# First output chunk of an expert inside its last products, six banks, column sums on GpSimd, reordered maxima

## The chip, the core and the metric

One of the eight cores of a Trainium2 chip runs the whole program. The metric is the device time of one execution in microseconds (us). Engines are named as the profile names them: PE is TensorE's matmul, PEld its weight load, DVE VectorE, ACT ScalarE, POOL GpSimd, SP SyncE (here it only issues DMAs).

## What is computed

Banded attention over 2 batches, 8 heads, 768 positions and width 64, whose output is read as 1536 tokens of width 512. Then a mixture of 8 experts, in which every token goes through every expert. Its weights P come from eight rounds of row and column scaling. Then a second mixture, in which every token is given to one expert by a greedy matching with 192 places for each expert.

```python
# first mixture (x: 1536 x 512, w1: 8 x 512 x 1024, w2: 8 x 1024 x 512)
P = np.exp(logits)
for _ in range(8):
    P /= P.sum(1, keepdims=True) + 1e-09
    P /= P.sum(0, keepdims=True) + 1e-09
    P *= N / E
for e in range(E):
    h = np.maximum(x @ w1[e], 0.0)
    out += P[:, e:e + 1] * (h @ w2[e])
# second mixture: tokens in the order of their logits, cap = N // E for each expert
for e in range(E):
    out[assigned == e] = np.maximum(x[assigned == e] @ w1[e], 0.0) @ w2[e]
```

## The kernel before

**Precision.** Each factor of a large product is split into a high and a low half of type f16 after it was scaled by a power of two (`split_hi` on ACT, L814; `split_lo` on DVE, L817), and a product is three matmuls (high-high, high-low, low-high). The scale needs the largest magnitude of the matrix: `maxima` (L1142) loads each matrix once more in eight pieces of 128x512 ("looks"), measures them in turn on ACT (L882) and DVE (L1195), and `settle` (L1199) spreads the result over the partitions by a small matmul (L134) into the bank `PGB` and forms the scale. All lists of such jobs go by `jobs` (L1349 to L1368), and `maxima` may run `AHEAD` = 3 jobs ahead of the splits.

**Stages.** Attention, then the hidden layer of expert 0 as 24 groups of 12 matmuls (L1418, `mm3`, L868 to L870; relu on ACT, L861 and L862, low half on DVE, L863). Beside its last groups run the eight rounds of scaling (L908 to L921): eight DVE operations a round, and the column sum as a matmul with ones (L918) into the bank `bc`. `bc` has the pool tag `misc`, which has one buffer, and so has `PGB` (L1412). Then, for experts 1 to 7, the hidden layer by one level of Strassen's scheme in Winograd's form: `hidden` (L1509) runs six `Set`s (two feature parts y, three token blocks tb), each with seven products of 12 matmuls of 256 columns (L1477). A product into a bank must wait until what lies there has been read: product 3 goes to the bank Y, which the DVE step L1540 reads after product 6. Experts 3 and 4 (`HB` and `HB + 1`) run as one list of twelve sets. The weights for it are in `WS`, one buffer: the parts of expert e + 1 (`kind == "fast"`, L1257; sums of blocks on POOL, L1281 to L1300) may be written only when expert e's sets with the same y are done, which the key `("hidden", e, y)` tells. After the hidden layer, `out_step` (L1599) runs the second product of the expert in 12 chunks of 128 tokens (24 matmuls of 512 columns, L1451) and adds each to `acc` by one DVE step (L1458). It needs W2 of the expert (`"plain"`, L1316 to L1343, tile `wslot`, one buffer), which may be written once the last chunk of the expert before is done. Chunks 0 to 10 stand behind the hidden layer, chunk 11 behind the first products of the next (`beside`). Expert 3's hidden values are put away in HBM, and its chunks as well as all 12 of expert 7 are held back.

**Order.** From L1618 on each engine follows the order of the program (`in_order`). Side work (splits, maxima, gate projections) stands in generators, and `pump` (L1397), which is called between the matmuls, lets them go on: each call adds credit for ACT, DVE and POOL (`CYCLE` in the hidden layer, `CHUNK` in the chunks), and a step is put into the program when its cost is covered. `pause(n)` and `ready` wait for a count that each call raises by 3. `have(key)` puts the side work into the program at once, credit or not, until the key is there.

**Tail.** After `late_logits` (L1057: the gate logits of experts 3 and 7 from their hidden values) come seven rounds of matching (L1746), whose latency is filled with the 24 chunks that were held back: `run(n)` puts n steps of three matmuls (L1668) into the program, eight steps a chunk, 24 steps a round. What is left is run at L1873. Then the second mixture.

Of the kernel before, what the change touches and what calls it, by code (L numbers as in the profile page):

```python
# [20 lines left out]
P = 128  # L21
# [21 lines left out]
def tile_sparse_attention_moe_moe(ctx, tc, q, k, v, ng, nl, wg1, w11, w12, wg2, w21, w22, out, taps=None):  # L43
# [864 lines left out]
    for it in range(8):  # L908
# [49 lines left out]
    AHEAD, SLACK, LAG2 = 3, 20, 28  # L958
    PEEKS = {1: 1, 2: 2, 3: 1, 4: 2, 5: 1}
    now = [0]  # L960
    LAG = 22

    def project(items, when=None):
# [42 lines left out]
        for k in range(-1, n + 1):  # L1006
# [3 lines left out]
            yield 1, 0  # L1010
# [8 lines left out]
            if fresh:  # L1019
                while not when(ahead.c):  # L1020
                    yield None
                yield 1, 0
                m = measure(ahead)
# [4 lines left out]
            yield 0, 2 if here else 0.7  # L1028
# [4 lines left out]
            if fresh:  # L1033
                yield 0, 1.2
                rescale(ahead, m, pt)
# [17 lines left out]
    def partial_logits(e):  # L1053
        yield from project([SimpleNamespace(src=acc[:, c, :], s=None, dst=L[:, c, :], plus=L[:, c, :], c=c, fetch=None)
                            for c in range(NC)], lambda c: ("added", e, c) in done)

    def late_logits(e, tb, plus, beside=None):  # L1057

        while e not in VG:
            yield None  # L1060
# [81 lines left out]
    def maxima(jobs):  # L1142

        n = 8 * len(jobs)
# [3 lines left out]
        def look():  # L1148
            while looks and nxt[0] < n:
                g = nxt[0]  # L1150
                w = source(*jobs[g // 8])
# [13 lines left out]
        for k, (kind, e, which) in enumerate(jobs):  # L1165
            if k < nxt[0] // 8 and 8 * k not in held:
                continue
            while k > at[0] + AHEAD:
                yield None
            if kind == "gate":  # L1170
                while jobs.index(("back", e, which)) not in scales:
# [8 lines left out]
                yield from project([SimpleNamespace(g=8 * k + f, s=scales[jobs.index(("back", e, which))], dst=V[:, f, :], plus=None, fetch=fetch)  # L1180
# [9 lines left out]
            settling.append(Stream(settle(k, jobs[k], am)))  # L1190

    def measured(t, am, a):
        yield (0, 1) if a % 2 else (1, 0)
# [5 lines left out]
    def settle(k, job, am, slack=SLACK):  # L1199
# [7 lines left out]
        yield 0, 1.3  # L1207
        scales[k] = rest()

    def weights(jobs):  # L1210
# [30 lines left out]
        if not wide:  # L1241
# [8 lines left out]
            yield from settle(0, jobs[0], am, 12)  # L1250
        for place, k in enumerate(real):
            kind, e, which = jobs[k]
            at[0] = k
            while k not in scales:
                yield None
            s = scales[k]
            if kind == "fast":  # L1257
                for y in range(NY):
                    while e > 1 and ("hidden", e - 1, y) not in done:
# [19 lines left out]
                    yield 1, 2, 4  # L1279
# [3 lines left out]
                    his((2, b22))  # L1283
                    yield from pause(9)
                    yield 1, 1
                    los((2, b22))
                    his((4, b11))
                    yield from pause(3)
                    yield 1, 1, 2
                    los((4, b11))  # L1290
                    nc.gpsimd.tensor_tensor(b11, b22, b11, op=ALU.subtract)  # L1291
                    his((6, b12))
                    yield from pause(8)
                    yield 1, 1
                    los((6, b12))
                    his((5, b11))
                    yield from pause(3)
                    yield 0, 1, 2
# [742 lines left out]
```

## Time and profile before

| | us |
|---|---|
| median of three runs | 1348.01 (1346.95 to 1348.44) |
| the profiled execution, its own time | 1346.19 |
| its span, first to last instruction | 1344.4 |
| PE busy in the span | 1257.6 (94%) |
| DVE busy | 896.9 (67%) |
| ACT busy | 757.5 (56%) |
| POOL busy | 208.6 (16%) |

The rows below come from this one execution. A row of the order of time begins with start and length in us, then engine, line, operation, output and inputs, and in brackets how long the engine had stood idle before it and which instruction ended that. "xN" joins N instructions of one kind. [...]

### The profile page before, as it was taken

Reading aid. Unit: us, or ns where it says so; the run is one execution under the profiler, and the core shown is the slowest. Engines: PE = TensorE matmul, PEld = TensorE weight load, DVE = VectorE, ACT = ScalarE, POOL = GpSimd, SP = SyncE. Lnnn points to the kernel's source line nnn. Section 1 sums busy time; section 2 is a strip of 40 time slices with the busy share of each in tenths; the row PEclk is TensorE's granted clock in tenths of the full one; section 3 lists DMA queues with packets and bytes.
Section 4 is the critical chain, followed back from the end, with each engine's and each line's share of the span. In section 5 each row is a group of like instructions: output and inputs, shape, how many; then the busy total and the mean of one; then the engine's idle time right before and its main releaser. Section 6 shows DMA issues by size and latency. Waiting matters only on the chain.

```text
span 1344.4 us, 24604 instructions
## 1 busy us (share of the span) xinstructions
PE 1257.6 (94%) x9481; PEld 824.8 (61%) x9481; DVE 896.9 (67%) x2038; ACT 757.5 (56%) x1507; POOL 208.6 (16%) x256
## 2 busy tenths in 40 slices
PE   6899789999999999988999999999997999979998
PEld 4666334586478448877458646955794444457665
DVE  7866684777647744667747765676667898835771
ACT  5866342576346525657537654644564686725872
POOL 2643610401101200211200030020000000031000
PEclk9999989999999999989999999999998999989999
DMA  9540004475732573635687666223737125167760
GB/s 233 122 113 8 1 18 139 141 252 165 242 120 62 172 227 113 226 110 172 191 258 246 193 207 225 84 64 126 235 101 245 64 70 206 48 225 260 250 206 24
DMA packets 155509, 207.19 MB, mean 154 GB/s; under 512 B 56448, under 2 KB 89216, under 8 KB 154240
## 3 DMA queue, kind: packets, MB, share of 16 engines
q1 hardware_dynamic: 153040, 193.04, 45.3%
q0 software_dynamic: 1920, 6.29, 1.3%
q10 hardware_dynamic: 432, 6.29, 1.1%
q8 instruction: 74, 1.21, 0.4%
q14 instruction: 43, 0.35, 0.1%
HBM read 174.13 MB, written 31.46 MB: 153 GB/s over the span
## 4 chain that ended last, share of the span: by engine, by line
PE 69%; issue 12%; DVE 10%; ACT 5%; DMA 2%; POOL 2%; POOLq 0%; SPq 0%; ACTq 0%; DVEq 0%
PE pX L1451 22%; PE pY L1477 9%; PE py L1668 8%; PE pX L1477 7%; PE pV L1477 4%; PE pZ L1477 3%; PE pY L1451 2%; PE pZ L1451 2%; PE ph L868 2%; PE ph L870 2%; PE ph L869 1%; DVE hslot L1498 1%; PE pr L1792 1%; DVE xt L1782 1%; DMA raw<-in_moe_w_dram 1%
## 5 line engine op out<-in xcount | busy, mean ns | idle before, releaser
L1477 PEld LDWEIGHTS <-ws 128*128 128x128 f16 x3528 | 346.2, 98 | 64.8 <-issue 20.7
L1451 PE MATMUL pX<-wslot,hslot 128*128 128x512 f16 x1440 | 317.2, 381 | 5.3 <-ACT wslot L814 2.7
L1451 PEld LDWEIGHTS <-hslot 128*128 128x128 f16 x1728 | 168.5, 98 | 203.7 <-issue 9.8
L1668 PE MATMUL py<-wslot,hslot 128*128 128x512 f16 x576 | 135.1, 384 | 0.0
L1477 PE MATMUL pX<-xt,ws 128*128 128x256 f16 x1008 | 126.7, 275 | 2.1 <-ACT pY L1526 2.1
L1477 PE MATMUL pY<-xs,ws 128*128 128x256 f16 x1008 | 125.7, 274 | 2.0 <-DVE pZ L1555 2.0
L1281 POOL TENSOR_TENSOR raw<-raw 128x512 f32<-128x512 f32 x14 | 23.3, 1664 | 583.2 <-DVE ws L817 381.4
L1498 DVE TENSOR_TENSOR hslot<-relu,hslot 128x512 f16<-128x512 f32 x126 | 88.9, 729 | 37.2 <-ACT relu L1491 36.8
L814 ACT ACTIVATE ws<-raw,s 128x512 f16<-128x512 f32 x98 | 68.3, 718 | 49.1 <-POOL raw L1291 14.7
L1668 PEld LDWEIGHTS <-hslot 128*128 128x128 f16 x576 | 53.6, 99 | 64.8 <-issue 9.4
L817 DVE SCALAR_TENSOR_TENSOR ws<-raw,s,ws 128x512 f16<-128x512 f32 x98 | 84.7, 886 | 10.3 <-ACT ws L814 10.3
L1458 DVE SCALAR_TENSOR_TENSOR acc<-pX,pf,acc 128x512 f32<-128x512 f32 x50 | 37.4, 749 | 71.7 <-PE pX L1451 71.7
L882 ACT ACTIVATE wide<-raw 128x512 bf16<-128x512 f32 x83 | 52.1, 627 | 50.5 <-DMA raw<-in_moe_w_dram 50.0
L1477 PE MATMUL pY<-xt,ws 128*128 128x256 f16 x504 | 63.3, 276 | 12.3 <-DVE s L1540 12.3
L817 DVE SCALAR_TENSOR_TENSOR w2slot<-raw,S,w2slot 128x512 f16<-128x512 f32 x72 | 51.6, 748 | 28.1 <-ACT w2slot L814 27.5
L868 PE MATMUL ph<-xt,w2slot 128*128 128x192 f16 x256 | 62.8, 248 | 6.3 <-ACT relu L862 5.0
L1488 ACT ACTIVATE hslot<-s 128x512 f16<-128x512 f32 x42 | 26.5, 630 | 68.3 <-DVE s L1540 68.2
L1195 DVE TENSOR_REDUCE wam<-raw 128x1 f32<-128x512 f32 x85 | 57.6, 677 | 10.3 <-DMA raw<-in_moe_w_dram 10.1
L814 ACT ACTIVATE w2slot<-raw,S 128x512 f16<-128x512 f32 x72 | 49.2, 722 | 25.1 <-DMA raw<-in_moe_w_dram 20.2
L870 PE MATMUL ph<-xt,w2slot 128*128 128x192 f16 x256 | 62.7, 246 | 0.0
L869 PE MATMUL ph<-xt,w2slot 128*128 128x192 f16 x256 | 62.7, 246 | 0.0
L1477 PE MATMUL pV<-xs,ws 128*128 128x256 f16 x504 | 62.3, 274 | 0.0
(337 smaller groups left out, 2342.5 us busy)
## 6 DMA issues: line engine op xcount, KB each, us to landing
raw<-in_moe_w_dram SPq DMA_DIRECT2D x299, 256.0 KB, 3.4
raw<-in_moe_w_dram SPq DMA_DIRECT2D x60, 512.0 KB, 5.1
relu<-in_moe_w_dram SPq DMA_DIRECT2D x85, 256.0 KB, 2.9
pre<-spill SPq DMA_DIRECT2D x56, 256.0 KB, 4.2
w2slot<-pre SPq DMA_DIRECT2D x4, 2048.0 KB, 8.6
hd<-hslot SPq DMA_DIRECT2D x12, 512.0 KB, 5.2
hslot<-hd SPq DMA_DIRECT2D x12, 512.0 KB, 5.6
w2slot<-pre ACTq DMA_DIRECT2D x3, 2048.0 KB, 15.3
```

What stands on the lines that cost most here:

```text
L814: nc.scalar.activation(hi, raw, AF.Copy, scale=s[:, 0:1])
L817: nc.vector.scalar_tensor_tensor(lo, raw, s[:, 0:1], hi, op0=ALU.mult, op1=ALU.subtract)
L868: nc.tensor.matmul(out_, lhs(0, a), rhs(0, a), start=a == 0, stop=False)
L869: nc.tensor.matmul(out_, lhs(0, a), rhs(1, a), start=False, stop=False)
L870: nc.tensor.matmul(out_, lhs(1, a), rhs(0, a), start=False, stop=a == n - 1)
L882: return nc.scalar.activation(t, src, AF.Abs, accum_out=dst)
L1195: nc.vector.tensor_reduce(am[:, a:a + 1], t, axis=AX.X, op=ALU.max, apply_absolute_value=True)
L1451: nc.tensor.matmul(flat(ps), h[:, y1, f, t * P:t * P + P], w[:, y2, f, :], start=f == 0 and n == 0, stop=f == FC - 1 and n == 2, skip_grou ...
L1458: nc.vector.scalar_tensor_tensor(acc[:, c, :], flat(ps), pf[:, c:c + 1], acc[:, c, :], op0=ALU.mult, op1=ALU.add)
L1477: nc.tensor.matmul(bank[:, u, :], self.w[:, z1, m, c, u * P:u * P + P], x[:, z2, c], start=first and u == 0 and c == 0 and n == 0, stop=c ...
L1498: nc.vector.tensor_sub(lo, r, hi)
L1668: pin(nc.tensor.matmul(ps, h[:, y1, f, t * P:t * P + P], w[:, y2, f, :], start=f == 0 and n == 0, stop=f == FC - 1 and n == 2))
```

## The change

- **Column sums.** L918 on PE becomes one `partition_all_reduce` on POOL, from SBUF to SBUF; the step after it reads SBUF in place of the bank.
- **Chunk 0.** `hidden` gets a call `between`, which runs chunk 0 of the same expert in the last turn of the loop, ahead of the last product 3. For expert 7 two chunks (0 and 1) are now done at this place and behind it; ten are held back.
- **Banks.** The chunks take turns over six banks (X and Y of both parities, V, Z).
- **Weights.** Parts 0, 1, 4 and 5 of the next expert wait for a new key `("early", e, y)`, set after product 5 of the last token block; only parts 2, 6 and 3 wait for `("hidden", e, y)`.
- **Maxima.** The scale of expert 4's first weights is measured ahead of three other jobs (`order`) and may run 6 ahead (`FAR`).
- **Credits.** Costs of small steps go from about 1 to 0.6, and from about 2 to 1.1 or less; `CHUNK` from (0.85, 0.75) to (0.6, 0.5), `CYCLE` from (0.33, 0.38) to (0.28, 0.32); expert 7 no longer has rates of its own.
- **Tail.** All late logits of expert 7 go through the side work (`after` is called for the last two sets too), W2 of expert 7 is loaded beside its first products, and the two calls of `late_logits` behind the loop are gone. Chunk 0 of expert 7 waits until the projection of expert 6 is in the program.

```diff
-        pt = misc([P, E], name="bc")
-        nc.tensor.matmul(pt, ones, pc, start=True, stop=True)
-        nc.vector.tensor_scalar(cs, pt, 1e-9, float(E) / NT, op0=ALU.add, op1=ALU.mult)
+        nc.gpsimd.partition_all_reduce(cs, pc, P, bass_isa.ReduceOp.add)
+        nc.vector.tensor_scalar(cs, cs, 1e-9, float(E) / NT, op0=ALU.add, op1=ALU.mult)
...
-            while k > at[0] + AHEAD:
+            while jobs.index(job) > at[0] + (FAR if kind == "fast" else AHEAD):
                 yield None
...
     def measured(t, am, a):
-        yield (0, 1) if a % 2 else (1, 0)
+        yield (0, 0.6) if a % 2 else (0.6, 0)
...
-                    while e > 1 and ("hidden", e - 1, y) not in done:
+                    while e > 1 and ("early", e - 1, y) not in done:
...
+                    while e > 1 and ("hidden", e - 1, y) not in done:
+                        yield None
+                    yield 2, 0
+                    his((2, b22), (6, b12))
+                    yield from pause(3)
+                    yield 0, 2
+                    los((2, b22), (6, b12))
                     after(2 * y)
...
+    order = list(jobs)
+    x = ("fast", HB + 1, 0)
+    order.remove(x)
+    order.insert(order.index(("gate", HB, 1)), x)
...
-    GROUP, CHUNK, CYCLE = (0.5, 0.5, 0.6, 3), (0.85, 0.75, 1.1, 3), (0.33, 0.38, 0.6, 3)
-    LAST, cycle = (0.3, 0.35, 0.6, 3), list(CYCLE)
+    GROUP, CHUNK, CYCLE = (0.5, 0.5, 0.6, 3), (0.6, 0.5, 1.1, 3), (0.28, 0.32, 0.6, 3)
+    cycle = list(CYCLE)
...
                 s.product(5, s.Y)
+                if s.tb == NTB - 1:
+                    done.add(("early", s.e, s.y))
                 nc.vector.scalar_tensor_tensor(ZB, s.s5, 1.0 / HS1, s.Y, op0=ALU.mult, op1=ALU.add)
                 pump(*cycle)
+            else:
+                after(g)
+                between()
             if j:
                 j.product(3, j.Y)
...
         sets[-1].lower(1, 0, R21)
+        after(sets[-1])
...
         if c == 0:
-            have("plain", e)
+            if e == E - 1:
+                while ("logits", e - 1) not in done:
+                    pump(*cycle)
+            else:
+                have("plain", e)
             factors(e)
-        n = count[0] + c
-        expert_out(e, c, ZB if c == NC - 2 else YB[n % 2] if c == NC - 1 else XB[n % 2])
+        n = count[0] % 2
+        new, old = (XB[n], YB[n]), (XB[1 - n], YB[1 - n])
+        expert_out(e, c, (new[0], old[0], VB, new[1], ZB, new[0], old[0], VB, old[1], ZB, old[0], old[1])[c])
...
+    def beside(e):
+        out_step(e)
+        if e == E - 2:
+            t = wslot(1)
+            nc.sync.dma_start(t, spilled["back", E - 1, 1])
+            W[E - 1, 1] = view(t, 1), W[E - 1, 1][1]
...
-            hidden(make(es), lambda: out_step(prev), after)
+            hidden(make(es), lambda: beside(prev), lambda: out_step(es[-1]), after)
...
-            while len(outs_of[prev]) > 1 and prev < E - 1:
+            while len(outs_of[prev]) > (1 if prev < E - 1 else LEFT):
                 out_step(prev)
...
+            if e == E - 1 and c not in outs_of[e]:
+                continue
...
-    for tb in range(1, NTB):
-        finish(late_logits(E - 1, tb, True, run))
```

## Rows read from the trace of the kernel before

**Rows 1.** Page, first part: busy time, share of the span, instructions.

```profile
PE 1257.6 (94%) x9481; PEld 824.8 (61%) x9481; DVE 896.9 (67%) x2038; ACT 757.5 (56%) x1507; POOL 208.6 (16%) x256
```

**Rows 2.** Busy time by stretch: length, engines (instructions), then PEclk, DMA share, GB/s.

```profile
159.50:193.60 34.10, 25.44 (x107) 11.04 (x106) 29.04 (x75) 11.53 (x25) 13.85 (x9) 0.85 0.03 8
193.50:199.40 5.90, 2.15 (x10) 0.79 (x8) 4.49 (x17) 3.68 (x5) 0.00 (x0) 0.76 0.00 0
200.00:255.00 55.00, 55.00 (x250) 24.71 (x249) 31.51 (x42) 20.82 (x39) 13.30 (x8) 0.97 0.43 138
1016.00:1034.00 18.00, 11.77 (x158) 6.62 (x158) 11.42 (x45) 3.96 (x7) 0.50 (x4) 0.81 0.87 273
```

**Rows 3.** Order of time, PE, from the rounds of scaling to expert 0's first chunk.

```profile
165.66 0.59 PE L918 MATMUL bc<-pc,ones 128*128 128x8 f32 x2 [5.88 <-DVE pc L915]
...
195.06 0.22 PE L134 MATMUL pg<-identh,wam 128*128 128x128 bf16 x1 [0.26 <-DVE cs L919]
198.01 0.59 PE L1451 MATMUL pX<-wslot,hslot 128*128 128x512 f16 x1 [2.73 <-ACT wslot L814]
```

**Rows 4.** Order of time, DVE: one round of scaling, then W2 of expert 0.

```profile
188.80 0.17 DVE L919 TENSOR_SCALAR cs<-bc 128x8 f32<-128x8 f32 x1 [0.48 <-PE bc L918]
...
189.12 0.64 DVE L863 TENSOR_TENSOR hslot<-relu,hslot 128x512 f16<-128x512 f32 x1
...
191.82 0.17 DVE L919 TENSOR_SCALAR cs<-bc 128x8 f32<-128x8 f32 x1 [0.48 <-PE bc L918]
...
197.99 4.87 DVE L817 SCALAR_TENSOR_TENSOR wslot<-raw,s,wslot 128x1024 f16<-128x1024 f32 x4 [0.69 <-ACT wslot L814]
```

**Rows 5.** Order of time, POOL: the folds of the tokens, and its smallest operation.

```profile
145.88 4.59 POOL L1104 TENSOR_TENSOR acc<-xt 128x1024 f32<-128x1024 f16 x2 [6.45 <-ACT relu L862]
...
171.21 2.61 POOL L1110 TENSOR_TENSOR ws<-ws 128x512 f32<-128x512 f32 x2
...
1016.24 0.14 POOL L1705 IOTA rnk<- 128x8 f32 x1
```

**Rows 6.** Groups by line, PE, 200 to 1010 us: busy, mean ns, idle before, releaser.

```profile
L1477 PE MATMUL pY<-xt,ws 128*128 128x256 f16 x492 | 61.8, 276 | 10.8 <-DVE s L1540 10.8
```

**Rows 7.** Order of time, POOL and DVE at the end of expert 4's hidden layer.

```profile
633.68 1.71 POOL L1281 TENSOR_TENSOR raw<-raw 128x512 f32<-128x512 f32 x1 [28.27 <-DVE ws L817]
...
634.19 3.42 DVE L1498 TENSOR_TENSOR hslot<-relu,hslot 128x512 f16<-128x512 f32 x2
```

**Rows 8.** Order of time, DVE and PE where expert 4's sets follow expert 3's.

```profile
568.21 0.69 DVE L1195 TENSOR_REDUCE wam<-relu 128x1 f32<-128x512 f32 x1 [5.02 <-DMA relu<-in_moe_w_dram]
...
573.05 2.72 PE L1477 MATMUL pY<-xt,ws 128*128 128x256 f16 x12 [4.44 <-DVE s L1540]
...
587.27 0.22 PE L134 MATMUL pg<-identh,wam 128*128 128x128 bf16 x1 [2.43 <-DVE L L1091]
...
608.84 2.07 PE L1477 MATMUL pX<-xt,ws 128*128 128x256 f16 x12 [2.06 <-ACT pY L1526]
```

**Rows 9.** Order of time, DVE and PE, W2 of expert 5 and its first chunk.

```profile
756.58 1.47 PE L1477 MATMUL pY<-xt,ws 128*128 128x256 f16 x12 [0.69 <-DVE s L1540]
...
760.73 1.46 PE L1451 MATMUL pX<-wslot,hslot 128*128 128x512 f16 x6 [1.17 <-DVE wslot L817]
...
762.98 1.28 DVE L817 SCALAR_TENSOR_TENSOR wslot<-raw,s,wslot 128x1024 f16<-128x1024 f32 x1
```

**Rows 10.** Order of time, PE, from expert 7's last products to the end of the matching.

```profile
1014.60 1.47 PE L1477 MATMUL pY<-xt,ws 128*128 128x256 f16 x12 [1.51 <-DVE s L1540]
1019.64 0.52 PE L1070 MATMUL pg<-vg7hl,hslot 128*128 128x16 f16 x13 [3.57 <-DVE amax L122]
1027.65 0.56 PE L1070 MATMUL pg<-vg7hl,hslot 128*128 128x16 f16 x16 [1.27 <-DVE L L1091]
1033.41 1.52 PE L1753 MATMUL pw<-ident,rw 128*128 128x128 f32 x12 [1.39 <-DVE rw L1735]
...
1182.14 4.04 PE L1668 MATMUL py<-wslot,hslot 128*128 128x512 f16 x18
```

More of the change, by code (lines that the diff above doesn't have):

```diff
@@ L1027, in project @@
                 pt = spread(m[:, 2:3])
-            yield 0, 2 if here else 0.7
+            yield 0, 1.1 if here else 0.4
             if last:
@@ L1055, in partial_logits @@
                             for c in range(NC)], lambda c: ("added", e, c) in done)
+        done.add(("logits", e))
     def late_logits(e, tb, plus, beside=None):
+        yield None
         while e not in VG:
@@ L1140, in ready, with maxima @@
             yield None
-    def maxima(jobs):
-        n = 8 * len(jobs)
+    def maxima(order):
+        n = 8 * len(order)
         held = {}
@@ L1150, in look @@
                 g = nxt[0]
-                w = source(*jobs[g // 8])
+                w = source(*order[g // 8])
                 c, h = divmod(g % 8, w.shape[1] // 512)
@@ L1164, in maxima @@
         look()
-        for k, (kind, e, which) in enumerate(jobs):
+        for k, job in enumerate(order):
+            kind, e, which = job
             if k < nxt[0] // 8 and 8 * k not in held:
                 continue
-            while k > at[0] + AHEAD:
+            while jobs.index(job) > at[0] + (FAR if kind == "fast" else AHEAD):
                 yield None
             if kind == "gate":
-                while jobs.index(("back", e, which)) not in scales:
+                while ("back", e, which) not in scales:
                     yield None
@@ L1178, in fetch @@
                     yield from ready(begun, LAG2)
-                yield from project([SimpleNamespace(g=8 * k + f, s=scales[jobs.index(("back", e, which))], dst=V[:, f, :], plus=None, fetch=fetch)
+                yield from project([SimpleNamespace(g=8 * k + f, s=scales["back", e, which], dst=V[:, f, :], plus=None, fetch=fetch)
                                     for f in range(FC)])
@@ L1197, in measured, with settle @@
             absmax_bound(t, am[:, a:a + 1])
-    def settle(k, job, am, slack=SLACK):
+    def settle(job, am, slack=SLACK):
         kind, e, which = job
@@ L1206, in settle @@
         yield from pause(6)
-        yield 0, 1.3
-        scales[k] = rest()
+        yield 0, 0.6
+        scales[job] = rest()
     def weights(jobs):
@@ L1249, in weights @@
                 yield from measured(t[:, a % 2 * 512:a % 2 * 512 + 512], am, a)
-            yield from settle(0, jobs[0], am, 12)
+            yield from settle(jobs[0], am, 12)
         for place, k in enumerate(real):
@@ L1415, in tile_sparse_attention_moe_moe @@
     late.append(1)
-    ahead.append(Stream(maxima(jobs)))
+    ahead.append(Stream(maxima(order)))
     flow.append(Stream(weights(jobs)))
@@ L1507, in begin, with hidden @@
         nc.scalar.activation(s.s5, VB, AF.Copy, scale=HS1)
-    def hidden(sets, beside, after):
+    def hidden(sets, beside, between, after):
         n = len(sets)
```

39 lines of the change are left out of this document (15 added, 24 removed).

## The prediction

> **What bounds the kernel now.** I read the busy times first: PE works 94% of the span, no other engine above 67% [rows 1]. So only time in which PE stands still, or runs at the low clock, can be won, and the change must be costed gap by gap. The table of stages says where the gaps are not: from 200 to 255 us PE is busy 55.00 of 55.00 us [rows 2], a stretch of output chunks. It also gives the price of a matmul of 512 columns there: 55.00 / 250 = 0.22 us, so a chunk of 24 takes 5.3 us. Next I read PE's order of time for every row that has an idle time in brackets. Five places hold nearly all of them between 159 and 1190 us, and the change touches each.
>
> First, the rounds of scaling. Between 159.5 and 193.6 us PE is busy 25.44 of 34.10 us at a granted clock of 0.85, and in the 5.9 us behind it 2.15 [rows 2]. PE is in order, the column sum L918 stands among the groups of expert 0, and the first waits 5.88 us for DVE [rows 3]. Then the matmul L134, which gives the scale of W2, runs only at 195.06, behind the last reader of the column sums: its bank has the pool tag of theirs. So W2 is split late (DVE from 197.99 [rows 4]) and the first chunk starts at 198.01 after a wait of 2.73 [rows 3]. Second, the ends of the hidden layers: product 3 waits for L1540, 10.8 us in all [rows 6], 4.44 of it inside the list of experts 3 and 4 [rows 8]. Third, that list. Fourth, W2 of expert 5 [rows 9]. Fifth, the start of the matching [rows 10].
>
> **The change part by part.** The sum is made against the profiled execution's own time, 1346.19 us.
>
> *A, column sums.* Removed: 16 records of L918 and the shared bank. In the stretch from 159.5, 107 records less those 16 are 91 products of expert 0 [rows 2]; at 0.22 they take 20.0 us and end at 179.5, three preparing matmuls later 180.2. Against 198.0 that is a gain of at most 17.8 us, if W2 is split by then. Its scale no longer waits for the rounds, and its split costs DVE 4.87 us [rows 4], so this is possible. Added: eight sums on POOL. No row shows an operation of POOL across partitions. The nearest rows bound it at 0.14 us (the small iota) and 2.3 us (half of the pair of folds, 128x1024) [rows 5]. I take 2.0, near the large one, because the value of each partition has to reach all others. A gain below 0.14 is out, as a sum cannot cost less than POOL's smallest operation. A round takes 191.82 - 188.80 = 3.02 us now, 0.48 of it waiting for PE [rows 4]; the rest, 2.54, holds one L863. With 2.0 a round takes 4.5. The first sum is asked for at 165.6 [rows 3], so the eighth is there at 165.6 + 2.0 + 7 x 4.5 = 199.1, and the factors some 2.4 us later (201.5). Chunk 0 needs them only when its bank is used again, by chunk 5, at 180.2 + 5 x 5.3 = 206.7: five chunks cover it now, where two banks covered two. What may spoil it is DVE, which is in order: the step behind each sum waits, and behind it stand L863 of the groups and the low halves of W2, for which PE waits. If DVE's order holds one L863 a round as now [rows 4], the eight groups left take 8 x 4.5 = 36 us and the chunk starts at about 205, 7 us later than now. The order is made by the scheduler and not in the trace. Bounds -17.8 and +7; I take -10, nearer to the gain, because the groups no longer share PE's order with the sums, and so need not go one a round.
>
> *B, chunk 0 inside.* It puts 5.3 us of PE work between product 6 and product 3. DVE is late there by 10.8 - 4.44 = 6.4 us over the lists [rows 6, 8], for instance because two L1498 took 3.42 us beside two block sums of POOL [rows 7]. No single lateness outside the list of twelve comes near 5.3. Bounds -6.4 and 0 (if the chunk's own side work pushes DVE back as much); I take -6. The bank of chunk 0 is that of the other parity, long read, and costs nothing.
>
> *C, early weights and urgent maxima.* At 568 DVE waited 5.02 us for a look that had only just been loaded: the weights of expert 4 were not ready, the side work was put in at once, and its reads followed their loads too closely. This cost PE 4.44, and the rest of that rush 2.43 and 2.06 [rows 8], together 8.9. Four of seven parts can now be written about one set earlier. But the same splits still fall into the same sets on DVE, so I take -5; bounds -8.9 and 0.
>
> *D, W2 of expert 5.* Chunk 0 is now wanted where product 3 would start, at 756.58 - 0.69 = 755.9; it reaches the last quarter of W2 18 x 0.22 = 4.0 us later, at 759.9, and that is there at 762.98 + 1.28 = 764.3 [rows 9]: 4.4 us of waiting against the 1.17 shown and two smaller ones, some 1.8. If the splits come as now, +2.6; if what was saved in C brings them forward, -1.8; if the lower credits put them back by another 4 us, +7. I take +2.
>
> *E, tail.* From 1016 to 1034 PE has one chunk (5.3) and 128 small matmuls (some 3.5) to do in 18.0 us, at a granted clock of 0.81 [rows 2]: about 9 are lost, plus the 1.51 ahead of product 3 [rows 10]. Two chunks move ahead of the matching: chunk 0 covers the 1.51, chunk 1 the wait for the last relu. Of the 16 steps that leave the tail, 8 stood in this stretch and 8 at its end, where 18 matmuls ran 4.04 us behind everything else [rows 10]; the matmul work is the same. The late logits no longer wait for the bank (3.57) nor for each other (1.27). The chain from the last logits to the first transposes (1.39 today [rows 10]) stays and is less covered, and the end of the matching then waits for DVE's index arithmetic. Bounds -11 and -3; I take -7. W2 of expert 7 is loaded from SP's queue behind chunk 11 of expert 6; the looks queued behind it wait for that chunk, and no matmul waits for them. I cost it at nothing; if a split stood behind it, a chunk's 5.3 us.
>
> *F, credits.* Costs and credits fall together in the hidden layer, so the splits keep their pace. In the chunks they slow down, under ten chunks of cover (53 us). Nothing, except under D.
>
> Sum: -10 - 6 - 5 + 2 - 7 = -26, so 1320.2 for such an execution. The median of the runs shown is 1.8 above it (1348.01 against 1346.19): 1322.
>
> **The rivals.** *Slow sums, slower kernel.* The mechanism is that of A: DVE's order holds one L863 a round, and a sum is longer than the rows suggest. The chunk then starts at 168.6 + 8 x (2.54 + T). The other parts give 16, so the point from which the kernel is slower lies at a start of 214, T = 3.1 us. With T = 5 it starts at 229, 31 us late: 1348 - 16 + 31 = 1363. For it: 2.0 is a guess, and one L863 a round is what the row shows. Against it: the rows of POOL's plain work are all below 2.3, and both conditions must hold.
>
> *First sum late.* POOL is in order too, and its folds run until 171.21 + 2.61 = 173.8 [rows 5], 8.2 us behind the request. If they keep their place, the cover of 206.7 - 201.5 = 5 us takes most of it; if the low halves stand behind, all 8 count: 1330. [...]
>
> *W2 becomes the wait.* The lower credits bring W2 late to more than one chunk 0: +7 at expert 5 in place of +2, and some 5 at expert 1, which has the fewest spare sets: 1332. For it: D has no slack today.
>
> *All of it.* A at -17.8, B at -6.4, C at -8.9, D at 0, E at -9: 42 us, 1306.
>
> *It does nothing.* The gaps come back behind the chunks, because DVE, busy 29.04 of 34.10 us in the rounds [rows 2], is what bounds there: 1348.
>
> **How the numbers follow.** Forecast 1322 with its own range of 1312 to 1331: 0.45. First sum late (1330): 0.10. W2 (1332): 0.14. All of it (1306): 0.10. Nothing: 0.07. Slow sums: 0.14. The range goes from 1304 to 1345; it leaves out the slow sums and most of the case of nothing, about 2 in 10. Within 0.2%, 2.7 us, is about what a measurement of this kernel cannot tell from no change. Faster: 0.45 + 0.10 + 0.14 + 0.10 = 0.79; same 0.07; slower 0.14.
>
> **What would show it.** A: the start of the first chunk (L1451 before) near 180 to 190, the time of one sum on POOL, and whether any chunk waits for its bank. B: no idle time ahead of product 3 with L1540 as its releaser. C: no wait above 1 us between the sets of experts 3 and 4. D: the wait for W2 ahead of expert 5's chunk 0. E: the time from expert 7's last product to the first transposes of the matching, and no matmuls of the held chunks behind the inverse. A sum of over 3 us, or a first chunk after 205, would make the prediction wrong.

## The result, and the profile of the changed kernel

| | before | changed |
|---|---|---|
| median, us | 1347.48 (1346.18 to 1348.44) | 1324.14 (1321.99 to 1327.00) |
| ratio, 95% interval | 1 | 0.9829 (0.9808 to 0.9850) |
| profiled execution, own time | 1346.19 | 1324.13 |

Forecast was 1322. The sum is close, but its terms are not: A gave a third of what it was put at, and B and C together more than they were put at. The page's first part stands against [rows 1]:

```profile
PE 1245.2 (94%) x9465; PEld 819.7 (62%) x9465; DVE 889.4 (67%) x2038; ACT 754.1 (57%) x1507; POOL 207.0 (16%) x264
```

The span fell by 22.1 us (1344.4 to 1322.3), and PE's busy time by 12.4 of these (1257.6 to 1245.2); the other 9.7 us are idle time. PE lost the 16 records of the column sums, which by themselves were busy 3.5 us. Some 6.3 us are the clock (an estimate): the two traces show granted clocks of 1.00 and 0.50 alone; at 0.50 PE was busy for 34.4 us before and for 21.9 us in the changed kernel, and matmuls that came 0.43 us apart at 0.50 came 0.215 apart at 1.00 (the first groups behind the scale of W2, below). The rest, some 2.6 us, is not traced.

**Where it went.** I cut both executions at the same steps of the program: the start of expert 1, of the list of experts 3 and 4, of expert 5, of expert 7, and the first measure behind the matching. Busy time by stretch, before (columns: length, then busy time and instructions of PE, PEld, DVE, ACT and POOL, PEclk, which is the granted clock as a share of full speed, DMA share, GB/s):

```profile
261.49:505.85 244.36, 241.07 (x1692) 160.79 (x1691) 158.24 (x285) 130.58 (x252) 25.63 (x17) 1.00 0.56 177
505.85:700.03 194.18, 182.59 (x1498) 134.42 (x1497) 123.06 (x238) 110.12 (x219) 26.08 (x16) 0.97 0.56 179
700.03:952.50 252.47, 247.42 (x1788) 166.29 (x1787) 168.39 (x342) 140.06 (x274) 23.35 (x16) 1.00 0.53 168
952.50:1188.04 235.54, 224.21 (x1790) 131.19 (x1789) 186.96 (x486) 151.02 (x238) 8.68 (x28) 0.99 0.36 129
```

and the same stretches of the changed kernel:

```profile
258.06:501.36 243.30, 240.91 (x1691) 160.81 (x1690) 154.70 (x282) 128.45 (x248) 24.78 (x17) 1.00 0.53 168
501.36:682.70 181.34, 177.86 (x1499) 132.11 (x1498) 127.55 (x242) 109.49 (x222) 23.33 (x16) 1.00 0.61 201
682.70:936.38 253.68, 249.34 (x1801) 167.58 (x1800) 167.98 (x355) 143.69 (x282) 22.90 (x16) 0.99 0.57 178
936.38:1165.96 229.58, 222.62 (x1778) 130.59 (x1776) 183.09 (x473) 147.04 (x229) 8.57 (x28) 0.99 0.33 120
```

Up to expert 1 the gain is 3.4 us, in experts 1 and 2 it is 1.1, in the list of experts 3 and 4 12.8, in experts 5 and 6 a loss of 1.2, in expert 7 and the matching 6.0. What follows is unchanged (156.4 and 156.3). In the list, idle time fell from 11.59 to 3.48 and busy time from 182.59 to 177.86 for the same work. The reason for the second is the clock: in the list PE was busy at 0.50 for 9.2 us before and never in the changed kernel, and half of that is 4.6. In the kernel before, around the wait of 4.44 us that ends at 573 us [rows 8]:

```profile
560.00:568.00 8.00, 8.00 (x125) 7.34 (x123) 3.08 (x8) 4.11 (x9) 0.00 (x0) 1.00 0.78 241
568.00:576.00 8.00, 3.56 (x21) 2.48 (x19) 6.50 (x19) 2.97 (x7) 0.00 (x0) 0.75 0.56 208
576.00:588.00 12.00, 9.57 (x125) 8.10 (x124) 7.29 (x20) 5.87 (x12) 2.92 (x2) 0.88 0.64 221
```

The granted clock was 1.00 ahead of the wait and 0.50 from 572.0 to 578.8 us, that is for the last us of the wait and the 5.8 us of matmuls behind it. The twelve at 573.05 took 2.72 us [rows 8], a product in the changed kernel takes 1.47.

**The start of the chunks.** PE's order of time, against [rows 3]:

```profile
182.05 0.29 PE L134 MATMUL pg<-identh,wam 128*128 128x128 bf16 x1 [14.73 <-DVE wam L1204]
182.13 0.63 PE L868 MATMUL ph<-xt,wslot 128*128 128x512 f16 x1
...
197.65 10.52 PE L1459 MATMUL pX<-wslot,hslot 128*128 128x512 f16 x48
```

The first chunk (L1459 now) starts at 197.65, before at 198.01. The waits of the rounds became one of 14.73 us at L134, the scale of W2, with the groups queued behind it; and the first twelve matmuls behind it came 0.43 us apart, at a granted clock of 0.50, and those from 187.5 on 0.215, at 1.00. POOL's order of time shows the cause, against [rows 5]:

```profile
166.89 5.09 POOL L1105 TENSOR_TENSOR ws<-xt 128x1024 f32<-128x1024 f16 x2
177.76 0.43 POOL L917 PARTITION_ALL_REDUCE cs<-pc  x1 [5.79 <-issue]
```

The first sum was asked for at 166.06 (the end of DVE's L915 below). POOL had folds until 171.98, and then stood 5.79 us with no instruction and nothing that it waited for. A sum itself takes 0.43 us here and mostly 0.40 later. DVE waited with it, against [rows 4]:

```profile
164.56 1.14 DVE L913 TENSOR_TENSOR Pm<-Pm,rs 128x96 f32<-128x96 f32 x1
165.73 0.33 DVE L915 TENSOR_REDUCE pc<-Pm 128x8 f32<-128x96 f32 x1
...
178.22 0.17 DVE L918 TENSOR_SCALAR cs<-cs 128x8 f32<-128x8 f32 x1 [8.22 <-POOL cs L917]
...
181.88 0.11 DVE L1204 TENSOR_REDUCE wam<-wam 128x1 f32<-128x8 f32 x1
```

Between the last two rows stand, among others, four looks (L1197), and L1204 is what L134 waits for.

**The other places.** Product 3 waits no more for the block sum (L1548 now), against [rows 6]:

```profile
L1485 PE MATMUL pY<-xt,ws 128*128 128x256 f16 x504 | 62.8, 273 | 0.0
```

In the list of experts 3 and 4 the wait of 4.44 us is gone; two are left nearly as they were (2.43 and 2.06 before), against [rows 8]:

```profile
564.02 0.22 PE L134 MATMUL pg<-identh,wam 128*128 128x128 bf16 x1 [1.87 <-DVE L L1092]
...
595.98 1.47 PE L1485 MATMUL pX<-xt,ws 128*128 128x256 f16 x12 [1.62 <-ACT pY L1534]
```

Chunk 0 of expert 5 waits for W2, against [rows 9], PE and then DVE:

```profile
743.34 3.39 PE L1459 MATMUL pX<-wslot,hslot 128*128 128x512 f16 x8 [1.98 <-DVE wslot L817]
```

```profile
744.39 1.27 DVE L817 SCALAR_TENSOR_TENSOR wslot<-raw,s,wslot 128x1024 f16<-128x1024 f32 x1
```

And the tail, PE, against [rows 10]: product 3 of expert 7 and the first transposes of the matching have no wait ahead of them, and no held-back chunk stands behind the inverse.

```profile
1005.79 1.47 PE L1485 MATMUL pY<-xt,ws 128*128 128x256 f16 x12
...
1009.95 0.83 PE L1071 MATMUL pg<-vg7hl,hslot 128*128 128x16 f16 x27 [1.13 <-DVE hslot L1506]
1010.64 4.69 PE L1459 MATMUL pX<-wslot,hslot 128*128 128x512 f16 x21
1015.17 1.04 PE L1774 MATMUL pw<-ident,rw 128*128 128x128 f32 x8
```

### The profile page after: what moved, and what is told of

It is laid out like the page before. It is cut to its first block, busy times and chain, and to the rows that moved or that the text cites. A ratio compares the mean times of both kernels' runs of the same rounds, so it can differ in the third digit from the quotient of the medians.

```text
span 1322.3 us, 24576 instructions
## 1 busy us (share of the span) xinstructions
PE 1245.2 (94%) x9465; PEld 819.7 (62%) x9465; DVE 889.4 (67%) x2038; ACT 754.1 (57%) x1507; POOL 207.0 (16%) x264
## 4 chain that ended last, share of the span: by engine, by line
PE 68%; issue 11%; DVE 9%; ACT 6%; POOL 3%; DMA 2%; POOLq 0%; ACTq 0%; DVEq 0%
PE pX L1459 11%; PE pY L1485 10%; PE pX L1485 7%; PE pY L1459 7%; PE py L1691 6%; PE pZ L1459 5%; PE pV L1459 5%; PE pV L1485 4%; PE pZ L1485 3%; PE ph L868 1%; DMA raw<-in_moe_w_dram 1%; PE ph L869 1%; PE ph L870 1%; PE pr L1813 1%; ACT ex L610 1%
## 5 line engine op out<-in xcount | busy, mean ns | idle before, releaser
L1459 PEld LDWEIGHTS <-hslot 128*128 128x128 f16 x1776 | 173.3, 98 | 204.0 <-issue 7.0
L1459 PE MATMUL pX<-wslot,hslot 128*128 128x512 f16 x768 | 175.3, 384 | 2.0 <-DVE wslot L817 2.0
L1691 PE MATMUL py<-wslot,hslot 128*128 128x512 f16 x528 | 121.0, 379 | 0.0
L1283 POOL TENSOR_TENSOR raw<-raw 128x512 f32<-128x512 f32 x14 | 24.9, 1778 | 526.8 <-DVE ws L817 399.9
L1459 PE MATMUL pY<-wslot,hslot 128*128 128x512 f16 x432 | 97.0, 379 | 0.0
L817 DVE SCALAR_TENSOR_TENSOR ws<-raw,s,ws 128x512 f16<-128x512 f32 x98 | 77.7, 824 | 15.4 <-ACT ws L814 15.1
L814 ACT ACTIVATE ws<-raw,s 128x512 f16<-128x512 f32 x98 | 65.6, 716 | 37.6 <-POOL raw L1291 18.7
L1197 DVE TENSOR_REDUCE wam<-raw 128x1 f32<-128x512 f32 x84 | 56.8, 678 | 14.2 <-DMA raw<-in_moe_w_dram 14.2
L1459 PE MATMUL pV<-wslot,hslot 128*128 128x512 f16 x288 | 64.7, 379 | 0.0
L1459 PE MATMUL pZ<-wslot,hslot 128*128 128x512 f16 x288 | 64.4, 379 | 0.0
## 6 DMA issues: line engine op xcount, KB each, us to landing
w2slot<-pre SPq DMA_DIRECT2D x4, 2048.0 KB, 12.2
```

Source lines behind the costliest of these rows:

```text
L814: nc.scalar.activation(hi, raw, AF.Copy, scale=s[:, 0:1])
L817: nc.vector.scalar_tensor_tensor(lo, raw, s[:, 0:1], hi, op0=ALU.mult, op1=ALU.subtract)
L1197: nc.vector.tensor_reduce(am[:, a:a + 1], t, axis=AX.X, op=ALU.max, apply_absolute_value=True)
L1283: nc.gpsimd.tensor_tensor(b11, b12, b11, op=ALU.subtract)
L1459: nc.tensor.matmul(flat(ps), h[:, y1, f, t * P:t * P + P], w[:, y2, f, :], start=f == 0 and n == 0, stop=f == FC - 1 and n == 2, skip_grou ...
L1691: pin(nc.tensor.matmul(ps, h[:, y1, f, t * P:t * P + P], w[:, y2, f, :], start=f == 0 and n == 0, stop=f == FC - 1 and n == 2))
```

## Experiments

All were timed in three rounds beside the kernel before, so kernels are compared by their ratios to it (0.001 is 1.35 us). "First chunk" and "list" are read from the profiled execution, "list" being the time from the start of expert 3 to that of expert 5.

| kernel | median | ratio, interval | first chunk | list |
|---|---|---|---|---|
| before | 1347.48 | 1 | 198.01 | 194.2 |
| changed | 1324.14 | 0.9829 (0.9808 to 0.9850) | 197.65 | 181.3 |
| e1_warm | 1327.46 | 0.9857 (0.9839 to 0.9874) | 198.61 | 181.4 |
| e2_hold_last | 1322.79 | 0.9826 (0.9809 to 0.9843) | 194.63 | 181.6 |
| e3_hold_two | 1312.72 | 0.9757 (0.9739 to 0.9775) | 186.27 | 181.7 |
| e4_sums_alone | 1345.76 | 0.9991 (0.9979 to 1.0003) | 197.80 | 193.8 |
| e5_no_between | 1336.31 | 0.9913 (0.9883 to 0.9943) | 197.76 | 185.7 |
| e6_no_urgent | 1319.05 | 0.9789 (0.9773 to 0.9806) | 196.70 | 179.9 |
| e7_late_key | 1322.45 | 0.9817 (0.9801 to 0.9834) | 197.84 | 180.4 |
| e8_own_bank | 1327.34 | 0.9858 (0.9842 to 0.9875) | 195.44 | 181.5 |
| e9_neither | 1326.17 | 0.9839 (0.9823 to 0.9856) | 197.59 | 181.3 |
| e10_old_credits | 1333.41 | 0.9891 (0.9870 to 0.9912) | 199.40 | 181.1 |
| e11_both | 1309.88 | 0.9723 (0.9706 to 0.9739) | 186.46 | 179.3 |
| e12_none_of_three | 1327.28 | 0.9846 (0.9826 to 0.9866) | 199.12 | 182.9 |

### Part A: why was the first sum late?

**e1_warm**: is the delay paid once in a program, or at each change?

```diff
     nc.vector.memset(ones, 1.0)
+    warm = sml.tile([P, E], F32, name="cs")
+    nc.gpsimd.partition_all_reduce(warm, ones[:, :E], P, bass_isa.ReduceOp.add)
```

> One column sum more, of a constant, as POOL's first work of the program; the rest is the changed kernel. Theory (the delay of 5.79 us ahead of the first sum is paid at each change between POOL's ordinary work and its sums): the copies and folds in between bring the delay back, the first sum of the rounds again begins some 5.8 us behind the last fold (at 177.8 us), the first chunk at 197 to 199, the time within 2 us of the changed kernel, 1322 to 1326. Rival (the delay is paid once in a program): the first sum of the rounds begins right behind the fold at 172.0, the wait of PE falls from 14.7 to some 9 us, and the time to about 1318.

POOL, order of time:

```profile
168.96 5.09 POOL L1107 TENSOR_TENSOR ws<-xt 128x1024 f32<-128x1024 f16 x2
180.00 0.43 POOL L919 PARTITION_ALL_REDUCE cs<-pc  x1 [5.95 <-issue]
```

The delay is there again in full, 5.95 us behind the fold, although a sum had run before: it is paid at the change. The warm sum itself holds up attention (POOL's first scaling step begins at 16.36 in place of 11.02), so all these rows stand 2.1 us later. At the first chunk 0.96 of that is left; what else makes up the 3.3 us by which the median lies above the changed kernel's, and 1.5 above the theory's range, was not followed. The compiled order of POOL in the changed kernel has an instruction without operands ahead of the sums, and one ahead of the next ordinary work.

```
65 L1105 TENSOR_TENSOR ws<-xt 128x1024 x2
66 L917 ISA
67 L917 ISA cs<-pc 128x8 x8
68 L1283 ISA
69 L1283 TENSOR_TENSOR raw<-raw 128x512
```

Neither is in the order of time. Under the line of the sums (L917) the trace has two MODIFY_POOL_CONFIG of 6 ns in POOL's queue, at 171.9 and 172.0, where the delay begins, and under L1283 two of 88 ns at 206.4, behind the last sum. That the delay belongs to them is read from their place alone. The delay was 5.79 us in the changed kernel and 5.95 in e1, and e1 adds that POOL's ordinary work in between brings it back.

**e2_hold_last** and **e3_hold_two**: if the sum's lateness is what PE waits for, it can be taken away. The folds of the last token block (e2: `tb >= 2`) or of the last two (e3: `tb >= 1`) are put behind the sums on POOL, so that the delay begins earlier; in e3 it should fall into time in which POOL is idle.

```diff
-        nc.gpsimd.partition_all_reduce(cs, pc, P, bass_isa.ReduceOp.add)
+        summed = nc.gpsimd.partition_all_reduce(cs, pc, P, bass_isa.ReduceOp.add)
...
+            with tc.issue_after(summed.ins) if tb >= 1 else ExitStack():
-            nc.gpsimd.tensor_tensor(R[g], x[:, 0, KH * g:KH * g + KH], x[:, 1, KH * g:KH * g + KH], op=ALU.add)
+                nc.gpsimd.tensor_tensor(R[g], x[:, 0, KH * g:KH * g + KH], x[:, 1, KH * g:KH * g + KH], op=ALU.add)
```

> The changed kernel with the last token block's pair of folds put behind the eight sums on POOL. Theory (the first sum is late by 5.1 us of folds and 5.8 us of delay behind them, and PE's wait follows it one for one): the folds end at 166.9, the first sum begins at 172.7, PE's wait of 14.7 us falls to about 9.6, the first chunk begins at about 192.5 and the time is about 1319. Rival (DVE's own work, not the sum, sets the chunk): first chunk at 197 to 198, time within 1.5 us of 1324.

> The changed kernel with the folds of the last two token blocks put behind the eight sums. Theory (as before, and the delay runs while POOL is idle): the folds of the first block end at 157, the delay of 5.8 us is over by 163, the first sum begins at 166.1 when it is asked for, PE's wait falls from 14.7 to 3 or 4 us, the first chunk begins at 185 to 188 and the time is 1311 to 1315. Rival (the folds are only moved): some 16 us of folds behind the sums hold back the splits of the folded tokens and with them expert 1, which gives more than half of it back: 1319 or more. Rival (DVE sets the chunk): 1324.

e2, POOL, PE and DVE:

```profile
172.35 0.43 POOL L917 PARTITION_ALL_REDUCE cs<-pc  x1 [5.83 <-issue]
```

```profile
179.14 0.29 PE L134 MATMUL pg<-identh,wam 128*128 128x128 bf16 x1 [12.21 <-DVE wam L1205]
```

```profile
172.81 0.17 DVE L918 TENSOR_SCALAR cs<-cs 128x8 f32<-128x8 f32 x1 [5.75 <-POOL cs L917]
...
176.66 0.17 DVE L918 TENSOR_SCALAR cs<-cs 128x8 f32<-128x8 f32 x1
...
178.93 0.15 DVE L1205 TENSOR_REDUCE wam<-wam 128x1 f32<-128x8 f32 x1
```

The sum came when expected (172.35 against 172.7), but PE's wait fell to 12.2 and not to 9.6. DVE's order is made anew for each kernel, and here a second round stands between the first sum and L1205. So the theory of one for one was too simple: PE waits for the sum and for whatever DVE's order puts between it and the scale. The first chunk starts 3.0 us earlier, but the time is that of the changed kernel within the intervals.

e3, POOL, then PE:

```profile
162.75 0.43 POOL L917 PARTITION_ALL_REDUCE cs<-pc  x1 [5.66 <-issue]
165.85 0.40 POOL L917 PARTITION_ALL_REDUCE cs<-pc  x1 [2.68 <-DVE pc L915]
...
199.94 5.09 POOL L1106 TENSOR_TENSOR acc<-xt 128x1024 f32<-128x1024 f16 x2 [7.39 <-issue]
```

```profile
171.57 0.23 PE L134 MATMUL pg<-identh,wam 128*128 128x128 bf16 x1 [4.08 <-DVE wam L1205]
...
186.27 10.52 PE L1460 MATMUL pX<-wslot,hslot 128*128 128x512 f16 x48
```

The wait is 4.08 us and the chunk starts 11.4 us earlier. The folds run at 200 us, and expert 1 starts at 246.68 against 258.06, also 11.4 earlier, so nothing is given back there. At the end the gain is 9.7 us by the ratios (11.4 by the medians).

Holding the folds back did more than empty POOL's queue. DVE's order of time in e3:

```profile
159.91 0.26 DVE L913 TENSOR_TENSOR Pm<-Pm,rs 128x96 f32<-128x96 f32 x1
160.20 0.32 DVE L915 TENSOR_REDUCE pc<-Pm 128x8 f32<-128x96 f32 x1
```

Without folds beside it L913 takes 0.26 us in place of 1.14, and DVE asks for the first sum at 160.52, 5.5 us earlier than in the changed kernel. The delay is not hidden in full, for the sum begins at 162.75, 2.2 us after that. So the sum is 15.0 us earlier, by 5.5 us of earlier request and 9.5 us of shorter lateness (11.7 to 2.2); how much of the 11.4 each of the two brought is not separated. A's 10 us were there to be had: the folds, which stood in POOL's queue and beside which DVE's steps ran slowly, and the delay took them.

**e4_sums_alone**: the kernel before, and of the change only the column sums (the first hunk of the diff).

> The kernel before with only the column sums moved to GpSimd; nothing else of the change. Theory (the first sum is late, so that the move alone brings little): the first chunk begins at 196 to 200 and the time is 1344 to 1348, at most 3.4 us below the kernel before, which is what the changed kernel had gained when expert 1 began. Rival (the move was worth the 10 us of the prediction, and the other parts gave less than they seem to): about 1337.

PE, order of time:

```profile
185.35 0.29 PE L134 MATMUL pg<-identh,wam 128*128 128x128 bf16 x1 [16.41 <-DVE wam L1201]
...
209.51 2.75 PE L1450 MATMUL pX<-wslot,hslot 128*128 128x512 f16 x12 [1.19 <-DVE acc L1455]
```

Alone, A is worth 1.2 us (between a gain of 2.8 and a loss of 0.4). The third chunk waits 1.19 us for its bank, since two banks cover two chunks and the factors come late; with six banks no chunk of the changed kernel waits.

**e8_own_bank**: could the sums have stayed on PE, in the unused fourth part of the scales' bank?

```diff
-        nc.gpsimd.partition_all_reduce(cs, pc, P, bass_isa.ReduceOp.add)
-        nc.vector.tensor_scalar(cs, cs, 1e-9, float(E) / NT, op0=ALU.add, op1=ALU.mult)
+        pt = PGB[:, 3, :E]
+        nc.tensor.matmul(pt, ones, pc, start=True, stop=True, skip_group_check=True)
+        nc.vector.tensor_scalar(cs, pt, 1e-9, float(E) / NT, op0=ALU.add, op1=ALU.mult)
```

(`PGB` is allocated ahead of the rounds.)

> The changed kernel with the column sums on TensorE again, but into the unused fourth part of the bank of the scales, so that the matmul for the scale of W2 needs no bank that the rounds hold. Theory (in the kernel before the shared bank held up W2, and GpSimd was not needed to free it): the sums cost 0.5 us each, nothing waits for folds or for a delay, the scale of W2 is there at 172 to 182, the first chunk begins at 186 to 191 and the time is 1312 to 1318. Rival (the groups of expert 0 share PE's order with the sums, and lose there what the bank gives): first chunk at 196 to 200, 1322 to 1327.

PE, order of time:

```profile
192.68 0.22 PE L134 MATMUL pg<-identh,wam 128*128 128x128 bf16 x1 [0.26 <-DVE cs L920]
195.44 0.59 PE L1460 MATMUL pX<-wslot,hslot 128*128 128x512 f16 x1 [2.54 <-ACT wslot L814]
```

L134 still ran only behind the last reader of the sums, though its operand was there at 176.7: in the program it stands behind the eighth sum and waits for DVE. Here a part of the bank did not act as a bank of its own, so this run doesn't test the theory; whether sums on PE in a truly separate bank would do as well as e3 stays open.

### Parts B, C and F: what freed the lists?

**e5_no_between**: chunk 0 back behind the hidden layer.

```diff
-            hidden(make(es), lambda: beside(prev), lambda: out_step(es[-1]), after)
+            hidden(make(es), lambda: beside(prev), lambda: None, after)
```

> The changed kernel with chunk 0 of each expert back behind the hidden layer; all else as changed. Theory (the chunk hides the lateness of DVE ahead of the last product 3 of every list, and a wait there costs more than its own length because the clock is low behind it): the waits of product 3 for the block sum come back, 6 us or a little more over the lists, and 1 to 3 us of low clock: 1330 to 1333. Rival (the lower credits and the new order of the weights have made DVE early, so that the place of the chunk no longer matters): 1323 to 1326.

Groups of PE, 200 to 1010 us, and busy time by stretch (columns as above):

```profile
L1485 PE MATMUL pY<-xt,ws 128*128 128x256 f16 x498 | 61.9, 273 | 6.7 <-DVE s L1548 6.7
```

```profile
258.17:504.66 246.49, 242.58 (x1691) 161.22 (x1690) 153.33 (x282) 128.84 (x247) 24.78 (x17) 0.99 0.52 166
504.66:690.34 185.68, 179.71 (x1499) 132.53 (x1498) 130.07 (x244) 109.67 (x222) 23.78 (x16) 0.99 0.60 196
690.34:947.34 257.00, 249.87 (x1800) 167.54 (x1799) 166.50 (x347) 142.11 (x279) 23.78 (x16) 0.99 0.54 170
947.34:1181.39 234.05, 225.03 (x1779) 131.47 (x1777) 185.22 (x479) 148.53 (x233) 8.60 (x28) 0.98 0.35 123
```

6.7 us of waits at product 3 are back, close to the 6.4 that the prediction counted for B. But the profiled execution is 15.3 us longer than that of the changed kernel, 8.9 of idle time and 6.5 of busy time (the four stretches against the same four of the changed kernel); the medians differ by 12.2 and the ratios by 11.3. The busy time is the clock: in these stretches PE is busy at 0.50 for 20.2 us, in the changed kernel for 6.8, and half of the difference, which is what the upper level would save, is 6.7. The theory of a wait and its low clock holds; even its upper end of 9 was too low, in part because the last logits of expert 7 wait 3.24 us in e5 and 1.13 in the changed kernel.

**e6_no_urgent**, **e7_late_key**, **e9_neither** (both edits together): which half of C freed the list of experts 3 and 4?

```diff
-            while jobs.index(job) > at[0] + (FAR if kind == "fast" else AHEAD):
+            while jobs.index(job) > at[0] + AHEAD:
...
-    order.remove(x)
-    order.insert(order.index(("gate", HB, 1)), x)
```

```diff
-                    while e > 1 and ("early", e - 1, y) not in done:
+                    while e > 1 and ("hidden", e - 1, y) not in done:
```

> The changed kernel with the maxima in the order of the kernel before, 3 jobs ahead; the early key stays. Theory (it was the look loaded too late that made the wait of 4.44 us at 573 us in the kernel before, and the low clock behind it): a wait of 3 us or more comes back in the middle of the list of experts 3 and 4, this list takes 5 to 9 us longer and the time is 1329 to 1333. Rival (the early key alone freed that list): 1323 to 1326.

> The changed kernel with parts 0, 1, 4 and 5 of the weights waiting for the old key again, the last product 3 in place of product 5; the maxima stay reordered. Theory (the urgent maxima made the gain in the list of experts 3 and 4; the key moves writes by less than one set): 0 to 2 us slower, 1324 to 1326. Rival (the key matters, since four of seven parts come one set later and the rush ahead of expert 4 is back): a wait of 2 us or more between the sets of experts 3 and 4, 1328 to 1332.

> The changed kernel with both undone: the maxima in the order of before, 3 jobs ahead, and the old key for parts 0, 1, 4 and 5. Theory (either of the two is enough to keep the looks ahead of the splits, which is why undoing one alone cost nothing): the wait of 3 to 5 us for a late look comes back in the list of experts 3 and 4, which takes 5 to 9 us longer than in the changed kernel: 1329 to 1333. Rival (neither did it; the lower costs and rates, or the new order of the parts, freed that list): 1317 to 1324 and no wait above 2 us there.

e6, busy time of experts 1 and 2; then PE in the changed kernel:

```profile
257.10:497.45 240.35, 240.35 (x1692) 160.93 (x1691) 156.68 (x285) 129.70 (x250) 24.34 (x17) 1.00 0.54 174
```

```profile
443.50 0.17 PE L992 MATMUL pg<-wg2hl,xp 128*128 128x16 f16 x1 [1.44 <-DVE V L1003]
```

My theory fell twice. Without the reordered maxima the list is no longer but shorter (179.9 against 181.3), and the time falls by 5.4 us (0.9789 against 0.9829, where the intervals just don't overlap). The larger part of it lies ahead of the list: experts 1 and 2 take 240.35 us, in which PE is never idle, against 243.30 in the changed kernel, where PE waits for the gate projection (L992). That projection, for expert 3, is the first of four jobs that the change moved the looks at expert 4's weights ahead of; the same 240.35 come back in e11. Without the key, 180.4 and no difference that can be told. Without both, 181.3 and 1326.17, 1.3 us by the ratios, inside the intervals, and a time between the two ranges on record. The key is of use only where the maxima keep their old order (0.9789 against 0.9839, 6.7 us). DVE does wait for a late look in e6, 3.72 and 4.17 us, but PE loses 0.49 us behind the first and nothing behind the second: in this order little that PE needs stands close behind the look. In e7 and e9 no such wait is above 1.8 us.

**e10_old_credits** and **e12_none_of_three** (e9 and e10 together): was it the credits, which I had costed at nothing?

```diff
-    GROUP, CHUNK, CYCLE = (0.5, 0.5, 0.6, 3), (0.6, 0.5, 1.1, 3), (0.28, 0.32, 0.6, 3)
+    GROUP, CHUNK, CYCLE = (0.5, 0.5, 0.6, 3), (0.85, 0.75, 1.1, 3), (0.33, 0.38, 0.6, 3)
...
-        yield (0, 0.6) if a % 2 else (0.6, 0)
+        yield (0, 1) if a % 2 else (1, 0)
```

(and the other small costs of `project` and `settle` as before)

> The changed kernel with the costs and rates of the credits as before: 1 and 1.3 in place of 0.6 for a look and a scale, the rates of chunks and cycles back. Theory (costs that fell more than the rates let the looks run ahead, which the prediction costed at nothing): the list of experts 3 and 4 takes 4 us or more longer than the 181.3 us of the changed kernel, and the time is 1328 to 1334. Rival (credits change nothing on the path, as the prediction had it): 1321 to 1326.

> The changed kernel with three things undone together: the order of the maxima, the old key, and the costs and rates of the credits. Left of the change are the column sums, chunk 0 inside, the six banks, the tail and the new order of the parts of the weights. Theory (the reordered maxima and the cheaper credits each keep the look of expert 4's weights ahead, so that undoing one of them alone leaves the list of experts 3 and 4 as short as it is): DVE waits again 3 us or more for a look in that list, the list takes 187 to 192 us in place of 181.3, and the time is 1338 to 1344. Rival (none of the three matters there; the new order of the parts, with fewer and shorter pauses, frees it): the list takes 180 to 183 us, no wait for a look above 1.5 us moves PE, and the time is 1331 to 1336.

e10, busy time of experts 1 and 2; then PE:

```profile
259.81:507.71 247.90, 243.50 (x1692) 161.61 (x1691) 157.60 (x285) 130.85 (x253) 23.60 (x16) 0.99 0.53 170
```

```profile
749.99 0.29 PE L134 MATMUL pg<-identh,wam 128*128 128x128 bf16 x1 [4.58 <-DVE wam L1204]
```

e10 is slower by 8.4 us, within my range, but not where I said: the list takes 181.1. In the profiled executions experts 1 and 2 lose 4.6 us (247.90 against 243.30), experts 5 and 6 2.3, the part up to expert 1 and that of expert 7 1.7 each. The longest wait, 4.58 us, stands inside chunk 0 of expert 5, at the matmul for the scale of expert 6's first weights, whose looks came late. e12 has the list at 182.9 and takes 1327.28, less than either theory gave; no look in the list makes DVE wait 0.6 us.

So the old credits cost 8.4 us beside the reordered maxima and 0.9 (not measurable) without them and the key. Undone together, these edits of C and F cost 2.3 us, inside the intervals. The list stays short without them. Of its 12.8 us, chunk 0 inside accounts for 4.3 (e5), and the sums alone leave it at 193.8 (e4). The remaining 8.5 us fall, by elimination only, to what e12 also keeps: the new order of the weights' parts, with shorter pauses, which I think likeliest, the six banks and the edits of the tail. No kernel had one of these alone, and it stays open.

**e11_both**: e3 and e6 together.

> The folds of the last two token blocks behind the sums, and the maxima in the order of the kernel before with 3 jobs ahead; all else as changed. Theory (the two gains lie in different stretches, 150 to 260 us and 375 to 680 us, and add up): 1312.7 - 5.1 = 1307.6, between 1306 and 1310, the first chunk at 186. Rival (an earlier start of expert 1 takes the room that the looks had): 1311 to 1315.

1309.88, 1.1% below the changed kernel and 2.8% below the one before: the fastest version of all. The gains add up in the main (between e3 and e11 4.6 us by the ratios and 2.8 by the medians, against 5.4 for e6), and of the list's 179.31 us PE is busy for 177.58:

```profile
487.21:666.52 179.31, 177.58 (x1497) 132.01 (x1496) 128.12 (x237) 108.68 (x218) 24.07 (x16) 1.00 0.60 198
```

## Why the prediction was right, and where it was wrong

The time (1322 against 1324.14) and the sign were right, with errors that cancelled. Step by step, from the profiled executions:

- **A** failed: -10 was put down, the first chunk came 0.4 us earlier, expert 1 started 3.4 earlier, and alone the part gave 1.2 (e4). The step that failed is that 91 products end at 179.5: PE stood still for 14.73 us, from 167.3 to 182.05. (The count itself is off by little, since the stretch holds 14 records of the sums and 92 products; 0.2 us.) The rival "First sum late" describes what happened, up to its size: 5.9 us of folds and the 5.79, for which no row of before had a price. The banks did cover the factors, as forecast. What stood behind the first sum in DVE's order was not a low half but four looks and the scale of W2, and with that scale PE's groups. The time of one sum, taken as 2.0, is 0.40. That mistake was harmless, since a long sum was never what decided; so "Slow sums" was out from the first row. The gain of 10 was real but needed the folds out of the way (e3: 9.7 by the ratios).
- **B** was right in mechanism and short in size. The waits it removes were sized well (6.4 forecast, 6.7 back in e5); it is worth 11 to 12 us because much of the low clock also went (20.2 us of busy PE at 0.50 in e5, 6.8 with it), and because expert 7's chunk 0 covers the last logits (3.24 us of waiting in e5, 1.13 with it). The term that was mis-sized is the price of a wait, which I had set equal to its length in every part but E.
- **C** was wrong as a cause. Of the waits that its 5 us were read from, 4.44 us went, but 1.87 and 1.62 were left of 2.43 and 2.06, so its own sign, no wait above 1 us, did not come. The two edits that I credited give 1.3 (e9, not measurable), and one of them, the reordered maxima, costs 3 to 5 us in this company (e6, e11 against e3).
- **D**: +2 forecast. The wait came where it was placed, at 1.98 us in place of 1.17, though the sum by the rows gave 4.4 for it, and the two experts lost 1.2.
- **E**: -7 forecast, -6.0 in the stretch of expert 7 and the matching. No kernel tested it alone, and part of it is B (e5 lost 4.5 there).
- **F**: costed at nothing, 8.4 us beside the reordered maxima. "The splits keep their pace" looked at the splits; the credits also set how early the maxima run, and in e10 PE waits for their scales.

By stretches the forecast -10 (A), -9 (B, C, D) and -7 (E) came out as -3.4, -12.7 and -6.0.

## What to carry to other kernels

When work is moved to an engine that follows the order of the program, read what that engine does at the moment of the first call (here 5.9 us of folds), and look for a delay where its kind of work changes (here 5.79 us): both the queue and the delay must be over before the call, which here was done by reordering work that had slack. Price a stall of the bounding engine at its length plus what its clock loses behind it (in e5 8.9 and 6.5 us), which is read from busy time over the same work, not from idle time alone; take out first what the change no longer computes. In a schedule made by credits and priorities, undo each edit by itself: parts that look like one improvement can be paying for each other.

## What was not expected of the hardware

- The change from POOL's ordinary work to its sums cost 5.79 us in the changed kernel, 5.95 in e1, 5.83 in e2 and 5.66 in e3, and the fold behind the sums in e3 began 7.39 us after them with nothing to wait for. In e3 the delay ran from the end of the ordinary work, not from the request: POOL was done at 157.09 and the sum asked for at 160.52, and only 2.2 us of the 5.66 were felt.
- A sum of 128x8 values over all 128 partitions took 0.40 us on POOL in six of the eight rounds of the changed kernel (0.43 in the first, 1.36 in the fifth), about as long as the pair of matmuls on PE before (0.59 us in [rows 3], 0.39 at a granted clock of 1.00). DVE stood idle for it about as long, 0.53 us in the second and third rounds against 0.48 [rows 4].
- Some small DVE operations stretched beside POOL's folds: in e8, while folds ran (until 171.17), a step of 128x12 values took 1.69 us (0.16 in the next round), and one of 128x96 took 1.95 (0.25); a reduction of 128x96 between the two kept its 0.25. Taking the folds away from the rounds relieved DVE too, by 5.5 us up to the first sum (e3).
- Short waits of PE cost nearly as much again behind them: in e5, 8.9 us more of idle time came with 6.5 us more of busy time over the same matmuls, because more of them ran at a granted clock of 0.50 (20.2 us against 6.8).
